# A new placement of the first two and a half batches of an attention and MLP kernel

## The chip, the cores and the metric

The kernel runs on one core of a Trainium2 chip. The metric is the time of one execution in microseconds (us) on the device. The engines of the core are named as the profile names them: PE (TensorE, matrix products; PEld is its weight load), DVE (VectorE), ACT (ScalarE), POOL (GpSimd) and SP (SyncE, which only issues transfers). Each engine takes its instructions in the order in which they were recorded, and waits at one whose input isn't there.

## The reference

For each of 8 batches and 8 heads, 576 positions are pooled into 32 memories, the queries attend to these, and the joined heads go through a two-layer MLP with a squared ReLU.

```python
a = phi - np.max(phi, axis=2, keepdims=True)     # phi: batch, head, 576, 32
a = np.exp(a)
a = a / (np.sum(a, axis=2, keepdims=True) + 1e-09)
k_m = np.einsum('bhsm,bhsd->bhmd', a, k)
v_m = np.einsum('bhsm,bhsd->bhmd', a, v)
scores = scale * np.matmul(q, k_m.transpose(0, 1, 3, 2))
scores = scores - np.max(scores, axis=-1, keepdims=True)
attn = np.exp(scores)
attn = attn / (np.sum(attn, axis=-1, keepdims=True) + 1e-09)
x = np.matmul(attn, v_m)                          # heads joined: 4608 x 512
h = np.maximum(x @ w_in, 0.0)                     # 512 -> 2048
out = h * h @ w_out                               # 2048 -> 512
```

## The kernel before

The MLP is the main loop. It has 256 steps: 8 batches, two halves of 288 positions (`t`), and 16 blocks of 128 hidden units (`f`). A step is `ffn1` (6 products into a PSUM tile `h`, line 566), ReLU and square on ACT (lines 568, 572, 577) and DVE (574), a subtraction on POOL (579) that gives the low part `g_lo`, and, two or three steps later, `ffn2` (line 595, 12 products into four PSUM tiles `acc`). In the first 16 steps the blocks f = 0 to 3 are not split, and `ffn2` is line 587. Values are split into a high and a low part of a faster format, which is why everything has a `_hi` and a `_lo`. The attention is folded into the MLP: `attend` makes the weights `a_hi`, `a_lo` of one half, and `make_u` multiplies `w_in` by the memories of the batch, so that `ffn1` is `u` times `a`.

What isn't the main loop is cut into generators, each with a list of places. The loop counts half steps, two in a step; at each of them the generators whose next place has come record their next piece. So the list `plan` sets, for the first two and a half batches, the order of the instructions on each engine; batches 3 to 7 follow a fixed list. The pieces are: `fetch_w_in`, `fetch_w_out` (a transfer of 512 KB of weights, which arrive as the bits of 8-byte numbers), `decode_in`, `decode_out` (two conversions on ACT, lines 479 and 482; three operations on DVE, 484, 486 and 489; one addition, line 496, on DVE or POOL as the plan says), `split_out`, `task_exp` (the softmax of phi), `task_mem` (the memories), `task_attend`, `task_u`, `task_stream` (transformed weights back from memory) and `task_spin` (a product that nobody reads).

`attend` has three passes over 128x576 numbers that may stand on DVE or POOL: subtracting the maximum (line 401), dividing by the sum (412), and the low part (419). The table `on_gpsimd` says which of the three are on POOL, by batch and half.

A single PSUM tile `ps_m` serves all the side work: each taker must find it released. `make_u` holds it from its products (line 372) through the copy `u_hi` on ACT (456) to the subtraction `u_lo` on DVE (458).

Before the loop, the string `order` gives the sequence of the pieces of batch 0 ("s" and `spin` being products without a reader), and `loads` the sequence of the first transfers. Almost all transfers are issued by SP, one after the other.

Of the kernel before, what the change touches and what calls it, by code (L numbers as in the profile page):

```python
# [24 lines left out]
def attn_moe_kernel(ctx: ExitStack, tc: tile.TileContext, qT, kv, phi, w_in, w_out, outT):  # L25
# [111 lines left out]
    def spin(n, x):  # L137

        h = ps_h.tile([P, 512], F32, name="h")
        for _ in range(n):  # L140
            nc.tensor.matmul(h, x, ident[:, None, :].broadcast_to([P, 4, P]), start=True, stop=True)

    def spin_r(*xs):

        h = ps_h.tile([P, 512], F32, name="h")
        for x in xs:
            for _ in range(4):
                nc.tensor.matmul(h[:, :T], turn[:, :P], x, start=True, stop=True)
# [578 lines left out]
    loads = [  # L727
        (first_phi,),
        (first_kv, 0),
        (first_kv, 1),  # L730
        (fetch_w_in, 0, 1),
        (fetch_w_in, 0, 0),
        (task_q, 0, 0),
        (task_q, 0, 1),
        (fetch_w_in, 1, 0),
        (fetch_w_in, 1, 1),
        (fetch_w_out, 0),
        (fetch_w_out, 1),
        (fetch_w_out, 4),
        (task_phi, 1),  # L740
        (next_kv,),
        (fetch_w_out, 2),
        (fetch_w_out, 5),
        (fetch_w_out, 6),
        (task_kv, 1, 0),
        (fetch_w_out, 3),
        (fetch_w_in, 3, 0),
        (fetch_w_in, 3, 1),
        (task_q, 1, 0),
        (fetch_w_in, 2, 1),  # L750
        (fetch_w_out, 7),
        (fetch_w_in, 2, 0),
    ]
    later = 10
# [35 lines left out]


    plan = [
        ((29, 29, 31), decode_in, 4, 0, nc.gpsimd),
        ((48, 53, 54), decode_in, 6, 0, nc.gpsimd),
        ((61,), task_kv, 2, 0),
        ((0, 1, 1), decode_out, 0, nc.gpsimd, True),
        ((6, 8, 10), decode_out, 3, nc.gpsimd, True),
        ((38, 43, 45), decode_in, 4, 1, nc.vector),
        ((110, 115), split_out, 0),
        ((5,), task_q, 1, 1),  # L800
        ((20,), fetch_w_in, 6, 1),
        ((90,), task_kv, 2, 1),
        ((0, 0, 2, 2, 3, 4), lambda: start["a1"]),
# [1 line left out]
        ((78, 81), split_out, 1),
        ((0, 1, 2), decode_out, 1, nc.gpsimd, True),
        ((47, 47, 49), decode_in, 6, 1, nc.vector),
        ((38,), fetch_w_out, 10),
        ((8,), fetch_w_in, 5, 0),
        ((62, 62, 64), decode_in, 7, 0, nc.vector),  # L810
        ((58, 59, 60), decode_in, 7, 1, nc.gpsimd),
        ((90,), task_stream, 2, 0),
        ((45, 46, 46, 48, 48), decode_out, 8, nc.vector),
        ((73, 73, 74), task_u, 0, 3),
        ((100, 101, 101, 102, 104, 107, 108), task_attend, 2, 0),
        ((52,), fetch_w_out, 13),
        ((0, 2, 2), task_u, 0, 0, HC, 2 * HC),
        ((92,), task_q, 2, 1),
        ((64, 66, 67, 68, 70), decode_out, 12, nc.vector),
        ((8, 9, 15), decode_in, 3, 0, nc.vector),  # L820
        ((16,), fetch_w_in, 4, 0),
        ((100,), task_stream, 2, 1),
# [1 line left out]
        ((35, 41, 41), decode_in, 5, 1, nc.vector),
        ((67,), fetch_w_out, 15),
        ((54, 56, 56, 58, 62), decode_out, 9, nc.vector),
        ((14, 14, 14, 17, 18, 18, 20), task_attend, 1, 1),
        ((73,), task_q, 2, 0),
        ((36,), fetch_w_out, 9),
        ((27,), fetch_w_out, 8),  # L830
        ((71,), fetch_w_out, 14),
        ((147,), task_stream, 2, 2),
        ((29, 29, 33, 35, 35), decode_out, 7, nc.gpsimd),
        ((49,), task_phi, 2),
        ((21, 22, 24, 27, 30), decode_out, 5, nc.gpsimd),
        ((68, 71, 71, 75, 77), decode_out, 13, nc.vector),
# [3 lines left out]
        ((3,), task_spin, 1),  # L840
        ((57,), fetch_w_out, 12),
        ((12,), fetch_w_in, 4, 1),
        ((9,), fetch_w_in, 7, 0),
        ((3,), task_spin, 1),
        ((105, 105, 105), task_u, 2, 0),
        ((109,), task_stream, 2, 3),
# [1 line left out]
        ((3, 8, 8), decode_out, 2, nc.gpsimd, True),
        ((92, 98), split_out, 2),
        ((110, 111, 113), task_u, 2, 1),  # L850
        ((11, 11, 14), task_u, 1, 0),
        ((7,), fetch_w_in, 5, 1),
        ((50, 51, 55), task_u, 0, 2),
# [2 lines left out]
        ((74, 75, 77, 79, 83), decode_out, 14, nc.gpsimd),
        ((14, 16, 19), decode_in, 2, 0, nc.gpsimd),
        ((14,), fetch_w_in, 6, 0),
        ((83, 84, 84, 86, 86), decode_out, 15, nc.gpsimd),
        ((118, 118, 120), task_u, 2, 2),  # L860
        ((100, 120), split_out, 3),
        ((10, 10, 10, 11, 11, 12, 12), task_attend, 1, 0),
        ((51, 55, 55, 58, 61), decode_out, 10, nc.vector),
        ((62, 62, 64), task_u, 1, 2),
        ((2, 4, 5, 6, 6, 6), task_exp, 1),
        ((28, 28, 28), task_u, 1, 1),
        ((38,), fetch_w_out, 11),
        ((76, 77, 77), task_u, 1, 3),
        ((32, 33, 33, 35, 37), decode_out, 6, nc.vector),
        ((62, 62, 64, 68, 70), decode_out, 11, nc.vector),  # L870
        ((20, 21, 23, 29, 29), decode_out, 4, nc.gpsimd),
        ((8, 8, 9, 9), task_mem, 1),
# [123 lines left out]
```

## Time and profile before

| | |
|---|---|
| time, median of 3 runs | 739.28 us (738.86 to 742.27) |
| time of the profiled execution | 739.42 us |
| its span, first to last instruction | 737.6 us |
| PE, PEld busy | 98%, 89% of the span |
| DVE, ACT, POOL busy | 51%, 48%, 36% |
| mean granted clock of TensorE | 0.995 of full speed |

The span and the time differ by 1.8 us, which lie around the instructions. A busy share is an average: the three side engines are nearly full in the first 150 us, when all weights are decoded, and far from it later.

### The profile page before, as it was taken

How to read it: one execution, taken by the hardware profiler on the slowest of the kernel's cores; microseconds unless marked ns; L12 is line 12 of the kernel's file. 1: busy time of each engine (PE TensorE's matmuls, PEld its weight loads, DVE VectorE, ACT ScalarE, POOL GpSimd, SP SyncE). 2: the span in 40 equal slices, each digit the busy share in tenths (PEclk: the TensorE clock that was granted, in tenths of full speed). 3: DMA queues.
4: the chain of work that ended last, by engine and by line, in shares of the span. 5: the costliest groups of instructions: out<-in, count | busy, mean ns of one | idle time of the engine just before them, and what ended most of it. 6: DMA issues, size and time to landing. Idle time of an engine off the chain costs nothing.

```text
span 737.6 us, 15709 instructions
## 1 busy us (share of the span) xinstructions
PE 721.2 (98%) x6170; PEld 655.1 (89%) x6170; DVE 379.6 (51%) x764; ACT 351.6 (48%) x750; POOL 263.8 (36%) x333
## 2 busy tenths in 40 slices
PE   8889999999999999999999999999999999999997
PEld 4467789889899898999899999899889999999997
DVE  4986779974565455254543556254542555321211
ACT  3546878874543344343544345433443435443332
POOL 1433334353443234332433324242333333333332
PEclk9999999999999999999999999999999999999999
DMA  9993228414429019131481216530391314100000
GB/s 306 354 363 117 105 67 265 147 30 125 140 76 313 25 56 298 44 122 34 143 222 44 80 33 244 122 121 2 87 281 31 122 34 147 58 33 1 33 2 32
DMA packets 64409, 89.61 MB, mean 121 GB/s; under 512 B 3984, under 2 KB 54928, under 8 KB 60752
## 3 DMA queue, kind: packets, MB, share of 16 engines
q1 hardware_dynamic: 63344, 87.34, 37.0%
q10 hardware_dynamic: 992, 1.28, 0.5%
q8 instruction: 48, 0.79, 0.4%
q14 instruction: 25, 0.20, 0.1%
HBM read 74.97 MB, written 13.63 MB: 120 GB/s over the span
## 4 chain that ended last, share of the span: by engine, by line
PE 83%; DVE 10%; ACT 4%; issue 1%; DMA 1%; POOL 1%; ACTq 0%; DVEq 0%; POOLq 0%
PE acc L595 49%; PE h L566 24%; PE ps_m L372 5%; PE ps_m L303 2%; DVE tmp L486 2%; DVE tmp L489 2%; PE acc L587 1%; DVE tmp L484 1%; DMA e_sb<-in_phi 1%; ACT low L482 1%; DVE u_lo L458 1%; ACT tmp L479 1%; DVE tmp L496 1%; ACT g L572 1%; ACT r L568 1%
## 5 line engine op out<-in xcount | busy, mean ns | idle before, releaser
L579 POOL TENSOR_TENSOR g_lo<-g,g_hi 128x288 fp32r<-128x288 f32 x240 | 202.4, 845 | 405.2 <-DVE g L574 313.3
L595 PE MATMUL acc<-g_hi,wo 128*128 128x288 f32 x1920 | 307.3, 298 | 0.4 <-DVE o L607 0.3
L595 PEld LDWEIGHTS acc<-g_hi,wo 128*128 128x128 f32 x1920 | 271.6, 188 | 25.3 <-ACT r L568 18.3
L574 DVE TENSOR_TENSOR g<-h,r 128x288 f32<-128x288 f32 x217 | 98.7, 456 | 307.3 <-ACT r L568 301.5
L568 ACT ACTIVATE r<-h 128x288 f32<-128x288 f32 x256 | 104.9, 410 | 295.0 <-PE h L566 286.4
L595 PE MATMUL acc<-g_lo,wo 128*128 128x288 f32 x960 | 176.5, 295 | 0.6 <-POOL g_lo L579 0.6
L595 PEld LDWEIGHTS acc<-g_lo,wo 128*128 128x128 f32 x960 | 144.2, 188 | 0.9 <-POOL g_lo L579 0.9
L577 ACT ACTIVATE g_hi<-r 128x288 fp32r<-128x288 f32 x240 | 106.5, 444 | 19.8 <-ACT r L568 0.8
L566 PE MATMUL h<-a_hi,u_hi 128*128 128x288 f32 x512 | 114.5, 305 | 0.7 <-ACT r L568 0.7
L566 PE MATMUL h<-a_hi,u_lo 128*128 128x288 f32 x512 | 109.8, 296 | 0.3 <-DVE u_lo L458 0.3
L566 PE MATMUL h<-a_lo,u_hi 128*128 128x288 f32 x512 | 109.6, 295 | 0.0
L566 PEld LDWEIGHTS h<-a_hi,u_hi 128*128 128x128 f32 x512 | 82.7, 188 | 10.5 <-issue 6.1
L566 PEld LDWEIGHTS h<-a_hi,u_lo 128*128 128x128 f32 x512 | 82.1, 188 | 0.5 <-DVE u_lo L458 0.5
L566 PEld LDWEIGHTS h<-a_lo,u_hi 128*128 128x128 f32 x512 | 82.2, 189 | 0.0
L458 DVE TENSOR_TENSOR u_lo<-ps_m,u_hi 128x1024 fp32r<-128x1024 f32 (+1 forms) x33 | 38.8, 1176 | 11.8 <-ACT u_hi L456 11.7
L372 PE MATMUL ps_m<-w_sb,mem 64*32 64x512 f32 (+1 forms) x528 | 37.1, 588 | 1.3 <-DVE w_sb L496 0.9
L587 PE MATMUL acc<-g_hi,wo 128*128 128x288 f32 x128 | 34.5, 414 | 1.7 <-POOL wo L496 1.7
L456 ACT CAST u_hi<-ps_m 128x1024 fp32r<-128x1024 f32 (+1 forms) x33 | 32.3, 980 | 5.0 <-PE ps_m L372 3.0
L587 PEld LDWEIGHTS acc<-g_hi,wo 128*128 128x128 f32 x128 | 23.6, 193 | 10.3 <-POOL wo L496 2.5
L482 ACT ACTIVATE low<-wo 128x512 int32<-128x512 uint32 x32 | 21.6, 674 | 8.6 <-DVE w_sb L496 4.4
L489 DVE SCALAR_TENSOR_TENSOR tmp<-wo,tmp 128x512 int32<-128x512 int32 x32 | 24.4, 761 | 1.1
L479 ACT ACTIVATE tmp<-wo 128x512 f32<-128x512 f32 x32 | 21.5, 672 | 4.4 <-DMA wo<-in_w_in 2.7
(136 smaller groups left out, 485.1 us busy)
## 6 DMA issues: line engine op xcount, KB each, us to landing
w_sb<-w_f SPq DMA_DIRECT2D x24, 1024.0 KB, 5.7
out_t<-o SPq DMA_DIRECT2D x62, 144.0 KB, 1.9
wo<-in_w_in SPq DMA_DIRECT2D x16, 512.0 KB, 8.3
wo<-in_w_out SPq DMA_DIRECT2D x16, 512.0 KB, 6.7
q_sb<-in_q SPq DMA_DIRECT2D x28, 288.0 KB, 3.4
kvb<-in_kv SPq DMA_DIRECT2D x28, 256.0 KB, 6.6
tmp<-in_kv SPq DMA_DIRECT2D x18, 256.0 KB, 6.0
w_f<-w_sb SPq DMA_DIRECT2D x4, 1024.0 KB, 7.6
```

The source lines that it names most:

```text
L372: nc.tensor.matmul(bank(out, half)[M * pr:M * (pr + 1), :y.shape[-1]], mem[hs, x, pr], y, start=True, stop=True)
L456: nc.scalar.copy(u_hi[:, :, n0:n1], ps[:, :, :n1 - n0])
L458: nc.vector.tensor_tensor(out=u_lo[:, :, n0:n1], in0=ps[:, :, :n1 - n0], in1=u_hi[:, :, n0:n1].bitcast(F32), op=ALU.subtract)
L482: nc.scalar.activation(r, word(0, U32), AF.Copy, scale=2.0 ** -29)
L489: nc.vector.scalar_tensor_tensor(out=c, in0=word(1, I32), scalar=-0x40000000, in1=c, op0=ALU.bitwise_and, op1=ALU.bitwise_or)
L566: nc.tensor.matmul(h[:, :T], u[:, qd, fs], x[:, qd], start=(i == 0), stop=(i == len(todo) - 1))
L568: nc.scalar.activation(r, h[:, :T], AF.Relu)
L574: nc.vector.tensor_tensor(out=g, in0=h[:, :T], in1=r, op=ALU.mult)
L577: nc.scalar.activation(g_hi, r, AF.Square)
L579: nc.gpsimd.tensor_tensor(out=g_lo, in0=g, in1=g_hi.bitcast(F32), op=ALU.subtract)
L587: nc.tensor.matmul(acc[e][:, :T], wo[f][:, e * P:(e + 1) * P], g_hi, start=first, stop=last)
L595: nc.tensor.matmul(acc[e][:, :T], wo[f][:, w, e * P:(e + 1) * P], x, start=first and x is g_hi and w == 0, stop=last and x is g_lo,)
```

## The change

Four things are changed. The transfers of `loads` stand in another order, 15 in place of 10 of them ahead of the loop's start. The places of nearly all pieces in `plan` are new, with some of the decoding additions changed between DVE and POOL (POOL has 18 of them, before 16). By the table `on_gpsimd`, ten passes of the six attentions of batches 0 to 2 stand on POOL, before fourteen. And the 28 products in float32r (`spin_r`) that nobody reads are gone, with the copy of 128x768 that fed them; five more `spin` stand in their place. Steps 35 to 38 square on DVE and no longer on ACT (`SQ_ACT`), and `ffn2` of step 9 comes ahead of `ffn1` of step 11.

```diff
-    def spin_r(*xs):
...
-            nc.scalar.copy(turn.rearrange("p (c x) -> p c x", c=3), e_sb[:, :3])
...
-    on_gpsimd = {(0, 0): (0, 1, 2), (0, 1): (0, 1, 2), (1, 0): (0, 1, 2), (1, 1): (0, 1), (2, 0): (1, 2), (2, 1): (0,)}
+    on_gpsimd = {(0, 0): (1, 2), (0, 1): (2,), (1, 0): (2,), (1, 1): (0, 1), (2, 0): (0, 2), (2, 1): (1, 2)}
...
-            spin_r(*(turn[:, i:i + T] for i in (0, 1, 2, 4)))
+            spin(2, ident)
             spin(2, mx[:, :1].broadcast_to([P, P]))
...
-            spin_r(turn[:, 8:8 + T], turn[:, :2 * T:2], turn[:, :1].broadcast_to([P, T]))
-            spin(1, sm[:, :1].broadcast_to([P, P]))
+            spin(2, sm[:, :1].broadcast_to([P, P]))
...
-    SQ_ACT = 39
+    SQ_ACT = 35
...
-        "e e e e e m m d0 m m d0 s d0 a0 a0 a1 d1 d1 a0 a0 d1 u0 d2 a0 d2 u0 a0 u0 d3 d3 d2 s d3 s d3 a0"
+        "e e e e e m m d0 m m s d0 a0 a0 d1 a0 a1 a0 d0 d1 d1 u0 d2 a0 s s d2 s a0 u0 d3 a0 d3 u0 d3 s d3 d2"
...
-        ((136, 142, 142), task_u, 2, 3),
+        ((128, 137, 137), task_u, 2, 3),
...
-        ((22, 23, 23), decode_in, 3, 1, nc.gpsimd),
+        ((22, 24, 25), decode_in, 3, 1, nc.gpsimd),
...
-        for _ in range({2: 1, 6: 1, 7: 1, 10: 1}.get(k, 0)):
+        for _ in range({2: 1, 6: 1, 7: 1, 10: 1, 11: 1}.get(k, 0)):
```

The new kernel is shorter, so its line numbers are smaller by 7 to 10: line 383 there is 391 of before, 393 is 401, 403 is 412.

The order on DVE is shown first where the attention of the second half of batch 0 follows on the decoding of the first blocks of w_out; `st`, `mx` and `sm` belong to the attention, `tmp` and `wo` to the decoding, and `at<-e_sb` begins the softmax of phi of batch 1. Before:

```order
L396 TENSOR_REDUCE mx<-st 128x18
L484 TENSOR_SCALAR tmp<-tmp 128x512
L486 TENSOR_SCALAR tmp<-tmp 128x512
L489 SCALAR_TENSOR_TENSOR tmp<-wo_133,tmp 128x512
L484 TENSOR_SCALAR tmp<-tmp 128x512
L486 TENSOR_SCALAR tmp<-tmp 128x512
L489 SCALAR_TENSOR_TENSOR tmp<-wo_391,tmp 128x512
L406 TENSOR_REDUCE sm<-st 128x18
L407 TENSOR_SCALAR sm<-sm 128x18
L408 RECIPROCAL sm<-sm 128x18
L458 TENSOR_TENSOR u_lo_333<-ps_m,u_hi_332 128x2x256
L173 TENSOR_TENSOR at<-e_sb 128x512
```

And with the change:

```order
L388 TENSOR_REDUCE mx<-st 128x18
L393 TENSOR_TENSOR st<-st,mx 128x576
L475 TENSOR_SCALAR tmp<-tmp 128x512
L477 TENSOR_SCALAR tmp<-tmp 128x512
L480 SCALAR_TENSOR_TENSOR tmp<-wo_135,tmp 128x512
L449 TENSOR_TENSOR u_lo_327<-ps_m,u_hi_326 128x2x256
L398 TENSOR_REDUCE sm<-st 128x18
L399 TENSOR_SCALAR sm<-sm 128x18
L400 RECIPROCAL sm<-sm 128x18
L403 TENSOR_TENSOR st<-st,sm 128x576
L166 TENSOR_TENSOR at<-e_sb 128x512
L167 TENSOR_TENSOR phi_mx<-at 128x256
```

The two passes `st<-st,mx` and `st<-st,sm` now stand on DVE, and one decoding instead of two lies between the maximum and the sum; the other one (of w_out block 1) comes after the maximum of phi.

On SP, the loads around phi of batch 1 (`e_sb`), its k and v (`u_hi`, `u_lo` for one half of the heads, `kvb` for the other) and the weights (`wo`). Before, from w_out block 1 on:

```order
L466 DMA wo_391<-in_w_out 128x512
L466 DMA wo_393<-in_w_out 128x512
L155 DMA e_sb<-in_phi 128x4x256
L159 DMA e_sb<-in_phi 64x256
L272 DMA u_hi_397<-in_kv 128x512 x2
L272 DMA u_lo_398<-in_kv 128x512 x2
L272 DMA u_hi_399<-in_kv 64x512
L466 DMA wo_406<-in_w_out 128x512
L466 DMA wo_408<-in_w_out 128x512
L466 DMA wo_410<-in_w_out 128x512
L272 DMA kvb_87<-in_kv 128x4x128
```

With the change, from w_out block 3 on:

```order
L457 DMA wo_143<-in_w_out 128x512
L457 DMA wo_377<-in_w_out 128x512
L264 DMA u_hi_379<-in_kv 128x512 x2
L264 DMA u_lo_380<-in_kv 128x512 x2
L264 DMA u_hi_381<-in_kv 64x512
L148 DMA e_sb<-in_phi 128x4x256
L152 DMA e_sb<-in_phi 64x256
L457 DMA wo_390<-in_w_out 128x512
L457 DMA wo_392<-in_w_out 128x512
L457 DMA wo_394<-in_w_in 128x512
L457 DMA wo_396<-in_w_in 128x512
L264 DMA kvb_87<-in_kv 128x4x128
```

Phi of batch 1 has moved behind five more blocks of weights (four of w_out, one of w_in) and one half of k and v, and w_out block 1 behind phi.

On DVE again, at the start of batch 3: `phi_mx`, `at`, `top` and `e_sb` are its softmax of phi, `u_lo` the last part of `u` of batch 2, `den` the end of the memories of batch 3, which take the same PSUM tile `ps_m`. Before:

```order
L237 TENSOR_TENSOR top<-top 32x8 x3
L239 COPY top<-top 32x8 x3
L574 TENSOR_TENSOR g<-h,r 128x288
L241 COPY at<-top 128x256
L242 STREAM_TRANSPOSE phi_mx<-at 128x256
L245 TENSOR_TENSOR e_sb<-e_sb,phi_mx 128x1024
L248 TENSOR_TENSOR e_sb<-e_sb,phi_mx 64x256
L574 TENSOR_TENSOR g<-h,r 128x288 x2
L458 TENSOR_TENSOR u_lo_3012<-ps_m,u_hi_3011 128x1024
L574 TENSOR_TENSOR g<-h,r 128x288
L312 TENSOR_SCALAR den<-ps_m 128x2
```

With the change:

```order
L226 TENSOR_REDUCE top<-at 128x8
L449 TENSOR_TENSOR u_lo_2861<-ps_m,u_hi_2860 128x1024
L229 TENSOR_TENSOR top<-top 32x8 x3
L231 COPY top<-top 32x8 x3
L565 TENSOR_TENSOR g<-h,r 128x288
L233 COPY at<-top 128x256
L234 STREAM_TRANSPOSE phi_mx<-at 128x256
L237 TENSOR_TENSOR e_sb<-e_sb,phi_mx 128x1024
L240 TENSOR_TENSOR e_sb<-e_sb,phi_mx 64x256
L565 TENSOR_TENSOR g<-h,r 128x288 x3
L304 TENSOR_SCALAR den<-ps_m 128x2
```

The subtraction `u_lo`, with which `ps_m` is released, stood after the softmax and stands now ahead of most of it.

## Rows read from the trace of the kernel before

**Rows 1.** The page: busy time by engine, and the chain that ended last.
```profile
PE 721.2 (98%) x6170; PEld 655.1 (89%) x6170; DVE 379.6 (51%) x764; ACT 351.6 (48%) x750; POOL 263.8 (36%) x333
...
PE 83%; DVE 10%; ACT 4%; issue 1%; DMA 1%; POOL 1%; ACTq 0%; DVEq 0%; POOLq 0%
```

**Rows 2.** Waits of TensorE, whole span: total us, times, longest us.
```profile
PE acc L587 <- POOL wo L496: 1.7, 1, 1.7
PE ps_m L303 <- DVE u_lo L458: 1.6, 1, 1.6
...
PE h L566 <- ACT r L568: 0.7, 1, 0.7
PE acc L595 <- POOL g_lo L579: 0.6, 1, 0.6
```

**Rows 3.** Timeline of DVE, 28 to 50: start us, us, instruction, [idle before].
```profile
30.76 0.84 DVE L391 STREAM_TRANSPOSE st<-acc 128x288 f32<-128x288 f32 x2
...
32.76 1.26 DVE L486 TENSOR_SCALAR tmp<-tmp 128x512 int32<-128x512 int32 x1
...
40.28 1.37 DVE L174 TENSOR_TENSOR phi_mx<-at 128x256 f32<-128x256 f32 x1
```

**Rows 4.** Timeline of POOL, the same stretch.
```profile
38.53 1.16 POOL L412 TENSOR_TENSOR st<-st,sm 128x576 f32<-128x576 f32 x1 [2.33 <-DVE sm L408]
39.65 1.71 POOL L496 TENSOR_TENSOR wo<-tmp,low 128x512 int32<-128x512 int32 x1
```

**Rows 5.** Line 401 by engine: duration ns min/median/max, first and last start us.
```profile
L401 DVE TENSOR_TENSOR st<-st,mx x11: 748/749/759, 187.2 to 623.5; 128x576 f32<-128x576 f32 x11
L401 POOL TENSOR_TENSOR st<-st,mx x5: 1159/1199/1471, 19.5 to 205.1; 128x576 f32<-128x576 f32 x5
```

**Rows 6.** Line 486 of DVE, 0 to 150; columns as in rows 5.
```profile
L486 DVE TENSOR_SCALAR tmp<-tmp x30: 426/427/1528, 16.4 to 145.7; 128x512 int32<-128x512 int32 x30
```

**Rows 7.** Line 173 of DVE, whole span; columns as in rows 5.
```profile
L173 DVE TENSOR_TENSOR at<-e_sb x7: 679/682/1390, 38.9 to 575.0; 128x512 f32<-128x512 f32 x7
```

**Rows 8.** Timeline of ACT, the same stretch.
```profile
33.77 0.68 ACT L403 ACTIVATE st<-st 128x576 f32<-128x576 f32 x1 [0.32 <-POOL st L401]
```

**Rows 9.** Timeline of PE, 20 to 55.
```profile
23.73 2.32 PE L148 MATMUL h<-wo 128*128 128x288 f32 x12
...
26.75 1.88 PE L141 MATMUL h<-ident 128*128 128x512 f32 x4
...
42.15 0.57 PE L187 MATMUL ps_m<-ident,phi_mx 128*128 128x128 f32 x2 [2.37 <-DVE phi_mx L176]
...
44.81 2.56 PE L587 MATMUL acc<-g_hi,wo 128*128 128x288 f32 x8
...
48.10 1.32 PE L303 MATMUL ps_m<-kvb,e_sb 128*32 128x130 f32 x40
...
50.80 2.21 PE L587 MATMUL acc<-g_hi,wo 128*128 128x288 f32 x8
```

**Rows 10.** Busy time by stretch: PE, PEld, DVE, ACT, POOL, PEclk, DMA share, GB/s.
```profile
0.00:30.00 30.00, 25.28 (x272) 14.35 (x272) 19.20 (x37) 11.56 (x22) 9.79 (x22) 0.94 0.97 329
30.00:40.00 10.00, 7.48 (x40) 4.08 (x40) 9.76 (x16) 6.01 (x12) 3.99 (x4) 1.00 1.07 318
40.00:50.00 10.00, 7.85 (x122) 7.10 (x126) 7.82 (x12) 5.85 (x12) 4.05 (x3) 0.83 1.04 400
```

**Rows 11.** Tile kvb, 25 to 50: its loads, and issue to landing.
```profile
L272 SPq DMA_DIRECT2D kvb<-in_kv x5: 540/601/2526, 28.9 to 33.2; - x5
...
DMA to landing us min/median/max: 7.4/7.9/8.5
```

**Rows 12.** Timeline of PE, 80 to 102: two runs of line 372.
```profile
81.82 1.93 PE L372 MATMUL ps_m<-w_sb,mem 64*32 64x512 f32 x16
...
100.54 1.09 PE L372 MATMUL ps_m<-w_sb,mem 64*32 64x512 f32 x16
```

**Rows 13.** Timeline of PE, 242 to 250.
```profile
244.72 1.32 PE L303 MATMUL ps_m<-kvb,e_sb 128*32 128x130 f32 x40 [1.60 <-DVE u_lo L458]
```

More of the change, by code (lines that the diff above doesn't have):

```diff
@@ L141, in spin @@
             nc.tensor.matmul(h, x, ident[:, None, :].broadcast_to([P, 4, P]), start=True, stop=True)
-    def spin_r(*xs):
[L145 to L148, printed above, removed]
     def load_phi(b, nc_q=nc.sync):
@@ L729, in attn_moe_kernel @@
         (first_kv, 0),
+        (task_q, 0, 0),
         (first_kv, 1),
+        (fetch_w_in, 0, 0),
         (fetch_w_in, 0, 1),
-        (fetch_w_in, 0, 0),
-        (task_q, 0, 0),
+        (fetch_w_in, 1, 0),
         (task_q, 0, 1),
-        (fetch_w_in, 1, 0),
+        (fetch_w_out, 2),
+        (fetch_w_out, 4),
+        (fetch_w_out, 0),
         (fetch_w_in, 1, 1),
-        (fetch_w_out, 0),
-        (fetch_w_out, 1),
[L739 to L743, printed above, removed]
+        (fetch_w_out, 5),
+        (fetch_w_in, 3, 0),
+        (fetch_w_out, 3),
+        (fetch_w_out, 7),
+        (next_kv,),
+        (task_phi, 1),
+        (fetch_w_out, 1),
         (fetch_w_out, 6),
+        (fetch_w_in, 2, 0),
+        (fetch_w_in, 3, 1),
         (task_kv, 1, 0),
-        (fetch_w_out, 3),
-        (fetch_w_in, 3, 0),
-        (fetch_w_in, 3, 1),
         (task_q, 1, 0),
         (fetch_w_in, 2, 1),
-        (fetch_w_out, 7),
-        (fetch_w_in, 2, 0),
     ]
-    later = 10
+    later = 15
     for fn, *args in loads[:later]:
@@ L760, in attn_moe_kernel @@
     spin(3, ident)
-    turn = const.tile([P, 3 * NQ * P], F32R, name=f"wo{NFT - 1}")
     start = {
@@ L792, in attn_moe_kernel @@
     plan = [
[L793 to L803, printed above, removed]
@@ L804, in attn_moe_kernel @@
-        ((50,), fetch_w_in, 7, 1),
[L805 to L822, printed above, removed]
-        ((40, 45, 46), task_u, 0, 1),
[L824 to L836, printed above, removed]
-        ((13, 17, 19), decode_in, 2, 1, nc.vector),
-        ((33, 35, 42), decode_in, 5, 0, nc.vector),
-        ((80, 83, 83, 84, 85, 87), task_exp, 2),
@@ L840, in attn_moe_kernel @@
[L840 to L846, printed above, removed]
-        ((136, 142, 142), task_u, 2, 3),
[L848 to L853, printed above, removed]
@@ L854, in attn_moe_kernel @@
-        ((92, 92, 93, 93), task_mem, 2),
-        ((108, 109, 112, 112, 114, 116, 118), task_attend, 2, 1),
[L856 to L872, printed above, removed]
-        ((22, 23, 23), decode_in, 3, 1, nc.gpsimd),
+        ((92, 99), split_out, 2),
@@ new lines, in attn_moe_kernel @@
+        ((15, 17, 19), decode_in, 2, 0, nc.vector),
+        ((76, 77, 78), task_u, 1, 3),
+        ((28, 29, 30), task_u, 1, 1),
+        ((3,), task_spin, 1),
+        ((53, 56, 56, 60, 61), decode_out, 9, nc.vector),
+        ((60,), fetch_w_out, 15),
+        ((0,), fetch_w_in, 4, 1),
+        ((107,), task_stream, 2, 3),
+        ((35, 41, 43), decode_in, 5, 1, nc.vector),
+        ((92, 92, 93, 93), task_mem, 2),
+        ((29, 30, 31), decode_in, 4, 0, nc.gpsimd),
+        ((54, 57, 59), decode_in, 6, 0, nc.gpsimd),
@@ new lines, in attn_moe_kernel @@
+        ((0,), fetch_w_in, 5, 0),
+        ((23, 24, 26, 31, 32), decode_out, 5, nc.gpsimd),
+        ((0, 2, 2), decode_out, 0, nc.gpsimd, True),
+        ((67,), fetch_w_out, 14),
+        ((11, 11, 14), task_u, 1, 0),
+        ((8, 8, 9, 9), task_mem, 1),
+        ((2,), fetch_w_in, 7, 0),
+        ((3, 3, 5), decode_out, 1, nc.gpsimd, True),
+        ((47, 47, 48), decode_in, 6, 1, nc.gpsimd),
+        ((50,), fetch_w_in, 7, 1),
+        ((62, 62, 62), decode_in, 7, 0, nc.vector),
+        ((49,), fetch_w_out, 10),
@@ new lines, in attn_moe_kernel @@
+        ((98,), task_stream, 2, 0),
+        ((71, 72, 74), task_u, 0, 3),
+        ((14, 14, 14, 16, 18, 19, 20), task_attend, 1, 1),
+        ((40, 45, 46), task_u, 0, 1),
+        ((61,), fetch_w_out, 13),
+        ((22, 24, 25), decode_in, 3, 1, nc.gpsimd),
+        ((103,), task_q, 2, 1),
+        ((67, 68, 69, 71, 75), decode_out, 12, nc.vector),
+        ((99,), task_stream, 2, 1),
+        ((25,), fetch_w_out, 8),
+        ((118,), task_stream, 2, 2),
+        ((28, 28, 31, 35, 35), decode_out, 7, nc.gpsimd),
@@ new lines, in attn_moe_kernel @@
+        ((3,), task_spin, 1),
+        ((76,), task_q, 2, 0),
+        ((40, 43, 43), decode_in, 4, 1, nc.vector),
+        ((32, 35, 39), decode_in, 5, 0, nc.gpsimd),
+        ((7, 7, 8), decode_out, 3, nc.gpsimd, True),
+        ((65,), task_phi, 2),
+        ((85,), task_kv, 2, 1),
+        ((95, 100, 100, 101, 103, 106, 109), task_attend, 2, 0),
+        ((0, 1, 2), task_u, 0, 0, HC, 2 * HC),
+        ((61, 61, 63), decode_in, 7, 1, nc.gpsimd),
+        ((10, 10, 10, 11, 11, 12, 12), task_attend, 1, 0),
@@ new lines, in attn_moe_kernel @@
+        ((61,), fetch_w_out, 12),
+        ((45, 46, 46, 48, 48), decode_out, 8, nc.gpsimd),
+        ((70, 71, 71, 78, 79), decode_out, 13, nc.gpsimd),
+        ((109, 109, 109), task_u, 2, 0),
+        ((74, 75, 77, 80, 83), decode_out, 14, nc.vector),
+        ((2,), fetch_w_in, 4, 0),
+        ((113, 113, 113), task_u, 2, 1),
+        ((59,), fetch_w_out, 11),
+        ((21,), fetch_w_in, 5, 1),
+        ((51, 56, 56, 58, 61), decode_out, 10, nc.vector),
+        ((97, 119), split_out, 3),
@@ new lines, in attn_moe_kernel @@
+        ((0, 7, 7), decode_out, 2, nc.vector, True),
+        ((81, 82, 82, 83, 83), decode_out, 15, nc.vector),
+        ((34,), fetch_w_out, 9),
+        ((76, 80), split_out, 1),
+        ((2,), fetch_w_in, 6, 0),
+        ((2, 4, 5, 6, 6, 6), task_exp, 1),
+        ((62, 63, 65), task_u, 1, 2),
+        ((62, 66, 66, 68, 70), decode_out, 11, nc.gpsimd),
+        ((32, 33, 33, 35, 37), decode_out, 6, nc.vector),
+        ((13, 17, 19), decode_in, 2, 1, nc.vector),
+        ((79, 82, 82, 84, 84, 87), task_exp, 2),
@@ L874, in attn_moe_kernel @@
+        ((8, 9, 17), decode_in, 3, 0, nc.vector),
+        ((77,), task_kv, 2, 0),
+        ((108, 109, 112, 112, 114, 116, 118), task_attend, 2, 1),
+        ((119, 122, 125), task_u, 2, 2),
+        ((36,), fetch_w_in, 6, 1),
+        ((104, 112), split_out, 0),
+        ((0,), task_q, 1, 1),
+        ((128, 137, 137), task_u, 2, 3),
+        ((0, 0, 2, 2, 6, 6), lambda: start["a1"]),
+        ((20, 21, 21, 29, 29), decode_out, 4, nc.gpsimd),
+        ((50, 50, 51), task_u, 0, 2),
     ]
```

## The prediction

> **What bounds the kernel now.** I read the page first. PE is busy for 98% of the span and makes up 83% of the chain that ended last; the rest of that chain is mostly DVE (10%) [rows 1]. So the time is PE's work plus what PE waits or runs slowly for. The change leaves the products of the main loop alone, so I looked for PE's losses and asked which of them the new placement reaches.
>
> The waits of PE [rows 2] are short, and of the long ones one stands early and one late: 1.7 us for the first decoded block of w_out, 2.37 us for the maximum of phi of batch 1 at 42.15 [rows 9], and 1.60 us at 244.72, where the memories of batch 3 want the PSUM tile that `u` of batch 2 still holds [rows 13]. The next ones are 0.7 and 0.6 us. One more is no wait in that view: the products of `u` that begin at 81.82 take 1.93 us, where the same ones take 1.09 us at 100.54 [rows 12]; the difference, 0.84 us, lies inside the group.
>
> The larger loss is the start. The stretch 30 to 40 has PE busy for 7.48 us, and 40 to 50 for 7.85 us at a mean granted clock of 0.83 [rows 10]. At the two levels of 1.2 and 2.4 GHz, 0.83 means about 3.4 of the 10 us at the lower one, which is 1.7 us of lost work; it stands behind the wait of 2.37 us. The engine that PE waits for there is DVE, busy for 9.76 of the 10 us from 30 to 40 [rows 10].
>
> Why is DVE so full? Its line 486 takes 0.43 us in the median and up to 1.53 [rows 6], line 173 takes 0.68 and once 1.39 [rows 7]. The long ones lie where POOL works: the maximum of phi, line 174, runs from 40.28 to 41.65 while POOL's addition runs from 39.65 to 41.36 [rows 3, 4]. At 32.76, line 486 takes 1.26 us [rows 3]. So a pass on POOL costs DVE up to 0.8 us while it runs, about as much as the 0.75 us for which DVE would do it itself, and on POOL it takes 1.20 us [rows 5].
>
> The Trainium skill says in "SBUF — State Buffer", section "Who interferes with whom", that the port pair is held for the whole instruction, and that whichever engine issues first blocks the other. This speaks against the change as well: a pass moved to DVE, with two inputs in SBUF, can hold up POOL's additions in turn. The trace agrees in one place, where POOL's addition takes 1.71 us [rows 4]. By that rule alone the four passes fewer on POOL would gain nothing at the start, and the sum below would lose its first term and come to 737.3.
>
> **The change part by part.** *Before 30.8 us: nothing.* The first half of batch 0 gets its subtraction on DVE, 0.75 us, in place of 1.20 on POOL and a hand-over; the exponential then starts when it did, since DVE does the same decoding meanwhile. The 12 products of `spin_r` that stood last took 2.32 us [rows 9]; in their place and in place of three spins behind them now stand six spins. Two take 1.88 us (four records, two to a product [rows 9]), so six take 5.6 us, against 2.3 + 2.8 before: `ffn1` of step 0 starts up to 1 us later. This is covered, because the next thing that PE needs is the decoded w_in from DVE, which comes at the same time: the transposition that follows it on DVE starts at 30.76 [rows 3], and I expect it there within 0.5 us. Without that cover it would cost the 1 us. The first half's low part may come 1 us later too, because its ACT copy stands behind a decoding whose weights now land later; it hides behind the same decoded w_in.
>
> *30.8 to 50.8: two limits.* First DVE. From 30.76 on it now does the transposition (0.84) and the maximum (0.75, as the pass has), the subtraction (0.75), one decoding (1.5, an estimate from three operations of which line 486 is one), then waits for the exponential. That was at 33.77 [rows 8]; two more activations stand ahead of it now, about 0.6 us each by the length of this one, so it ends near 35.6. The sum, reciprocal and second pass take 2 us: 37.6. DVE is then free for phi.
>
> Second, the transfers, which are saturated: 329, 318 and 400 GB/s in three stretches [rows 10]. Counted from `loads`, 12.32 MB stand in the queue up to the last part of `kvb` before, and 14.94 MB now. The last part was issued at 33.2 and took 7.4 us, so it landed at 40.6 [rows 11]; by the rates 13.3 MB had moved by then, 1.0 more than these. So now it lands when 15.9 MB have moved: 13.05 MB by 40, the rest at 400 GB/s, at 47.2. Phi of batch 1 (11.67 MB deep) lands in the same way near 38.7. Its maximum takes 0.68 us [rows 7] and two smaller operations of an estimated 0.4 without POOL beside it, so PE has it at 40.3 in place of 42.15: 1.9 us earlier. Then w_out block 1, which lands near 40.3, must be converted, decoded and added, 3.5 us, so `ffn2` of step 1 starts near 43.9 in place of 44.81 [rows 9], and the next `ffn1` is done about when the last `kvb` lands. The memories' products, which took from 48.10 to 50.80 [rows 9], end 1.4 us behind the last `kvb`: 48.6. That is 2.2 us earlier. If the transfers go on at 318 GB/s, `kvb` lands at 49.0 and 0.4 us are left; if the clock falls again, up to 1.7 us of work come on top, partly inside the wait for `kvb`. I take **2.0 us**, between 0 and 2.5; it is carried on, because the attention of batch 1 starts from these memories and its two moved passes are shorter.
>
> *50 to 240.* `u` of the second quarter waited 0.84 us for an addition of w_in. That addition is recorded two places later now (25 for 23), and the products at 28 as before, but POOL has two softmax passes fewer to do ahead of it. I take **0.4 us**, between 0 and 0.8. The two more additions on POOL, the four squares moved from ACT to DVE and all the new places can take away waits (0.7 + 0.6 us [rows 2] and smaller ones) or make new ones. No row shows them. Below stand the 1.3 us, above as much again and more; I take zero, since nearly every piece keeps its place within a few half steps.
>
> *244.* `u_lo` is recorded six half steps ahead of the memories of batch 3 in place of one (137 and 142, against 143). A copy and a subtraction don't reach over the three steps between, so the wait goes: **1.6 us**, or 0 if the transfer that feeds these products is late.
>
> *The rest* (batches 3 to 7) is the same list and costs the same.
>
> **Sum.** 739.42 - 2.0 - 0.4 - 1.6 = 735.4 in terms of the profiled execution, which lies 0.14 us above the median. Forecast: 735.3 us.
>
> **The rivals.** (a) *The forecast*, chance 0.45, with a range of its own of 733.5 to 736.8 (the first term from 1.0 to 2.5, the unknown waits 1 us either way).
> (b) *The load order eats the gain of the start.* Phi and w_out block 1 stand 3.3 MB and 4.9 MB deeper in the queue, and a rate of 318 GB/s, as from 30 to 40, is enough for it, or a clock that falls in the wait for `kvb`. Against it stands the 400 GB/s of the next stretch. Then 739.28 - 0.4 - 1.6 = 737.3; chance 0.2.
> (c) *The waits after 60 us go as well.* For it: they are short and each hangs on one placing. Then the 1.3 us and the other half of the 0.84 come off: 735.3 - 1.7 = 733.6, with a start that gains its full 2.5, 733.1; chance 0.2.
> (d) *The decoding becomes the bound, slower.* DVE already makes up a tenth of the chain that ended last and ACT 4% [rows 1], so where the chain lies on them, a longer one comes out of PE's time one for one. With 18 additions on POOL in place of 16, two more collisions of 0.8 us, and four more squares on DVE (an estimate of 0.4 each, half of a pass of [rows 5], which has twice the numbers): 3.2 us; if the chain doesn't start earlier either, 739.28 - 1.6 + 3.2 = 740.9. It is slower than before from a growth of 4 us over the forecast, and by over 0.5% from 7.8 us, which takes some five pieces late by one transfer. Chance 0.15, of which 0.09 beyond 0.5%.
> That the change doesn't do what it says is excluded: the rows of the order show the passes moved.
>
> **How the numbers follow.** Half a per cent, 3.7 us, is about what a measurement of this kernel can tell from no change: 735.6 and 743.0 are the limits. The forecast lies at the lower one; of its 0.45 I count 0.25 as faster and 0.2 as the same. With (c), faster is 0.45. The same: 0.2 + 0.2 from (b) + 0.06 from (d) = 0.46. Slower: 0.09. The range leaves out one in ten on each side: from 731.8, below (c) with some unknown waits gone, to 740.5, most of the way to (d).
>
> **What would show it.** Right: no wait of PE at 244; the maximum of phi reaching PE near 40.3; the products with `kvb` ending near 48.6, behind a wait for a transfer; line 486 at 0.43 us more often; the start of the first `ffn1` near 29. Wrong: a clock below 1.00 in more than one stretch after 20 us; waits of over 1 us of PE between 60 and 240, on ACT or POOL; `kvb` landing after 49.

## The result, and the profile after

The changed kernel takes 732.58 us in the median of 4 runs (732.32 to 733.08), the kernel before 739.15 beside it. The ratio is 0.990, interval 0.988 to 0.993: faster by 1.0%. The profiled execution took 732.32 us, 7.10 less than that of before. The gain is in three places, read from one event that both traces have, the ReLU of a step on ACT (line 568, after 559): at step 6 it starts 1.90 us earlier (59.22 for 61.12), at step 64 5.42 us earlier (218.17 for 223.59), and from step 72 to the end 7.10 us. So in this pair of profiles the start gave 1.9 us, the stretch from 60 to 224 us 3.5, and the beginning of batch 3 1.7.

The page of the changed kernel, parts 1 and 4, and its windows (PE, PEld, DVE, ACT, POOL busy, PEclk, DMA, GB/s); they answer to [rows 1, 10]:

```profile
PE 718.4 (98%) x6152; PEld 651.3 (89%) x6152; DVE 379.1 (52%) x771; ACT 350.0 (48%) x745; POOL 263.1 (36%) x330
...
PE 95%; DVE 2%; ACT 1%; DMA 1%; issue 0%; POOL 0%; ACTq 0%; DVEq 0%; POOLq 0%
```

```profile
30.00:40.00 10.00, 7.67 (x49) 4.94 (x50) 9.60 (x20) 6.75 (x14) 1.64 (x2) 1.00 1.06 355
40.00:50.00 10.00, 8.46 (x147) 6.47 (x146) 8.36 (x17) 6.22 (x12) 3.96 (x3) 1.00 1.07 324
```

Busy shares hardly move. What moves is the chain that ended last: PE from 83% to 95%, DVE from 10% to 2%. The timeline of PE after, for [rows 9, 12, 13]:

```profile
28.88 0.83 PE L557 MATMUL h<-a_hi,u_hi 128*128 128x288 f32 x2
...
39.19 0.38 PE L180 MATMUL ps_m<-ident,phi_mx 128*128 128x128 f32 x2
...
41.98 2.21 PE L578 MATMUL acc<-g_hi,wo 128*128 128x288 f32 x8 [0.36 <-POOL wo L487]
...
45.97 0.43 PE L295 MATMUL ps_m<-kvb,e_sb 128*32 128x130 f32 x8 [0.19 <-DMA kvb<-in_kv]
...
48.64 2.21 PE L578 MATMUL acc<-g_hi,wo 128*128 128x288 f32 x8
...
79.94 1.09 PE L364 MATMUL ps_m<-w_sb,mem 64*32 64x512 f32 x16
...
237.63 1.32 PE L295 MATMUL ps_m<-kvb,e_sb 128*32 128x130 f32 x40
```

The maximum of phi is there at 39.19 without a wait (before 2.37 us, at 42.15), the products with `kvb` end at 48.64, the products of `u` at 79.94 take 1.09 us in place of 1.93, and the memories of batch 3 wait for nothing. Waits of PE from 50 to 260, before and after (total us, times, longest):

```profile
PE ps_m L303 <- DVE u_lo L458: 1.6, 1, 1.6
PE h L566 <- ACT r L568: 0.7, 1, 0.7
PE acc L595 <- POOL g_lo L579: 0.6, 1, 0.6
PE acc L595 <- DVE o L607: 0.3, 1, 0.3
PE acc L595 <- ACT o L614: 0.2, 1, 0.2
```

```profile
PE acc L586 <- DVE o L598: 0.2, 1, 0.2
```

Without `u_lo`, which belongs to the beginning of batch 3, these rows name 1.6 of the 3.5 us in the middle (1.8 less the 0.2 that is left), and the products of `u` are 0.84. The other 1.1 us lie in no gap: from step 13 to step 64 PE stands idle for 1.75 us of 143.50 before and for 0.23 us of 139.90 after, so the rest of the difference is time in which the profile shows it busy, and which products take it was not located. The windows from 80 to 165, before and then after, show that the side engines do more in the same time, POOL most of all:

```profile
80.00:165.00 85.00, 83.25 (x621) 73.26 (x620) 69.52 (x108) 66.87 (x148) 35.58 (x35) 1.00 0.38 128
```

```profile
80.00:165.00 85.00, 84.77 (x652) 76.83 (x652) 72.51 (x113) 68.23 (x147) 43.57 (x45) 1.00 0.43 142
```

### The profile page after: what moved, and what is told of

Same layout as the page of the kernel before. It is cut to its first block, busy times and chain, and to the rows that moved or that the text cites. A ratio compares the mean times of both kernels' runs of the same rounds, so it can differ in the third digit from the quotient of the medians.

```text
span 730.5 us, 15675 instructions
## 1 busy us (share of the span) xinstructions
PE 718.4 (98%) x6152; PEld 651.3 (89%) x6152; DVE 379.1 (52%) x771; ACT 350.0 (48%) x745; POOL 263.1 (36%) x330
## 4 chain that ended last, share of the span: by engine, by line
PE 95%; DVE 2%; ACT 1%; DMA 1%; issue 0%; POOL 0%; ACTq 0%; DVEq 0%; POOLq 0%
PE acc L586 53%; PE h L557 28%; PE ps_m L364 6%; PE acc L578 4%; PE ps_m L295 2%; PE h L141 1%; DMA e_sb<-in_phi 1%; PE acc L295 0%; ACT tmp L470 0%; DVE tmp L480 0%; ACT low L473 0%; ACT r L559 0%; DVE tmp L477 0%; POOL w_sb L487 0%; DVE e_sb L202 0%
## 5 line engine op out<-in xcount | busy, mean ns | idle before, releaser
L570 POOL TENSOR_TENSOR g_lo<-g,g_hi 128x288 fp32r<-128x288 f32 x240 | 204.5, 854 | 393.5 <-DVE g L565 314.7
L565 DVE TENSOR_TENSOR g<-h,r 128x288 f32<-128x288 f32 x221 | 100.4, 456 | 303.5 <-ACT r L559 295.5
L578 PEld LDWEIGHTS acc<-g_hi,wo 128*128 128x128 f32 x128 | 23.2, 189 | 10.7 <-POOL wo L487 3.0
L410 POOL TENSOR_TENSOR a_lo<-at,a_hi 128x576 fp32r<-128x576 f32 x15 | 21.7, 1445 | 15.3 <-ACT a_hi L409 15.3
```

Of the source, the lines that this page charges most:

```text
L410: by(2).tensor_tensor(out=a_lo, in0=at, in1=a_hi.bitcast(F32), op=ALU.subtract)
L565: nc.vector.tensor_tensor(out=g, in0=h[:, :T], in1=r, op=ALU.mult)
L570: nc.gpsimd.tensor_tensor(out=g_lo, in0=g, in1=g_hi.bitcast(F32), op=ALU.subtract)
L578: nc.tensor.matmul(acc[e][:, :T], wo[f][:, e * P:(e + 1) * P], g_hi, start=first, stop=last)
```

## The experiments

Two theories for the start and the middle. The one of the prediction: fewer passes on POOL free DVE, and the phi transfer, early enough, does the rest. The rival: only the places in `plan` count, since they decide what stands ahead of what in each engine's queue.

### The passes alone, and the new plan alone

The kernel before with one line of the change:

```diff
-    on_gpsimd = {(0, 0): (0, 1, 2), (0, 1): (0, 1, 2), (1, 0): (0, 1, 2), (1, 1): (0, 1), (2, 0): (1, 2), (2, 1): (0,)}
+    on_gpsimd = {(0, 0): (1, 2), (0, 1): (2,), (1, 0): (2,), (1, 1): (0, 1), (2, 0): (0, 2), (2, 1): (1, 2)}
```

> The kernel before with only the new table of passes on POOL. Theory P (the passes freed DVE and with it the whole decoding, so they made the gain between 50 and 160 us): start 1.0 us earlier, middle 2.5 us shorter, about 735.5 us. Theory L (the new places in the list made that gain): the start gains at most 1.0 us, the middle nothing, 738.2 to 739.

Measured: 740.45 us, ratio 1.0007 (0.9995 to 1.0019). The passes alone give nothing that can be measured, and the trace suggests why. DVE's line 486, 0 to 60, grouped (instructions | busy us, mean ns | idle us before), and the window 0 to 60 (columns as above), of the kernel before and then, in the same two views, with the passes moved:

```profile
L486 DVE TENSOR_SCALAR tmp<-tmp 128x512 int32<-128x512 int32 x9 | 8.4, 934 | 0.3
```

```profile
0.00:60.00 60.00, 50.58 (x525) 32.22 (x525) 43.16 (x76) 28.97 (x55) 20.26 (x30) 0.94 0.97 331
```

```profile
L486 DVE TENSOR_SCALAR tmp<-tmp 128x512 int32<-128x512 int32 x9 | 6.8, 757 | 0.3
```

```profile
0.00:60.00 60.00, 51.34 (x524) 31.52 (x525) 43.17 (x81) 28.81 (x55) 15.44 (x26) 0.97 0.96 331
```

The collisions become fewer (934 to 757 ns in the mean), but DVE is busy for 43.17 us in place of 43.16: it does itself what it lost to them. The prediction took from the section of the Trainium skill that it names ("SBUF — State Buffer", "Who interferes with whom") that the passes would gain nothing. This run agrees in the result. It doesn't show the way that the prediction gave for it, that DVE holds up POOL's additions in turn: of the six additions up to 60 us one is long in either trace, 1.71 us before and 1.66 with the passes moved.

What decides when phi's maximum comes is the stretch on DVE that ends with it, from the transposition of the second half of batch 0 on. Its two ends before, with the passes moved, and in the changed kernel:

```profile
30.76 0.84 DVE L391 STREAM_TRANSPOSE st<-acc 128x288 f32<-128x288 f32 x2
...
41.68 0.42 DVE L176 TENSOR_TENSOR phi_mx<-phi_mx,e_sb 64x256 f32<-64x256 f32 x1
```

```profile
32.24 0.84 DVE L391 STREAM_TRANSPOSE st<-acc 128x288 f32<-128x288 f32 x2
...
42.91 0.42 DVE L176 TENSOR_TENSOR phi_mx<-phi_mx,e_sb 64x256 f32<-64x256 f32 x1
```

```profile
30.87 0.83 DVE L383 STREAM_TRANSPOSE st<-acc 128x288 f32<-128x288 f32 x2
...
38.58 0.42 DVE L169 TENSOR_TENSOR phi_mx<-phi_mx,e_sb 64x256 f32<-64x256 f32 x1
```

From the start of the one to the start of the other these are 10.9, 10.7 and 7.7 us. In the six traces of this document with two decodings in the stretch it is 10.7 to 10.9 us, in the eight with one 7.6 to 8.7, wherever the passes stand.

And the kernel before with the list `plan`, `SQ_ACT` and the place of one `ffn2`:

```diff
-        ((22, 23, 23), decode_in, 3, 1, nc.gpsimd),
+        ((22, 24, 25), decode_in, 3, 1, nc.gpsimd),
...
-    SQ_ACT = 39
+    SQ_ACT = 35
...
-        for _ in range({2: 1, 6: 1, 7: 1, 10: 1}.get(k, 0)):
+        for _ in range({2: 1, 6: 1, 7: 1, 10: 1, 11: 1}.get(k, 0)):
```

> The kernel before with only the new list of places (with steps 35 to 38 squared on DVE and ffn2 of step 9 ahead of ffn1 of step 11). Theory L: 3.5 us in the middle and 1.6 us at the start of batch 3 come off, about 734.2 us. Theory P: only the 1.6 us, about 737.5 us.

Measured: 732.55 us, ratio 0.989 (0.987 to 0.991). The list, with the two small edits, carries the whole gain, 1.7 us more than theory L, which gave it nothing at the start.

### The change with the old passes, and with the old load order

```diff
-    later = 15
+    later = 10
```

with `loads` in its old order in the second; in the first `on_gpsimd` of before.

> The changed kernel with the old table of passes. Theory P: 1 us lost at the start and 2.5 us in the middle, about 736 us. Theory L: up to 1 us at the start, partly behind the wait for the last kvb, nothing later, 732.6 to 733.6 us.

> The changed kernel with the old order of loads: phi, w_out block 1 and kvb of batch 1 land 9, 14 and 6 us earlier, so PE has no wait for kvb near 46. If the new order of loads is what limits its start: 0.7 to 1.2 us faster than the changed kernel, about 731.6 us. If the new order is needed by the new places (a decoding that waits for its weights): slower than the changed kernel, 734 us or more. If neither: 732.6 us.

Measured: 732.89 us, 0.989 (0.988 to 0.991), and 732.40 us, 0.989 (0.987 to 0.990). Neither part is needed. With the old load order the last `kvb` lands at 40.1 us and PE doesn't wait for it (with the new one at 46.7): step 6 lies 2.37 us ahead of before, with the new one 1.90.

### Half of the list

The new places of decoding and transfers alone (with their adder engines and the sequence of the new list), with the old ones of the computing pieces (`u`, `attend`, the softmax of phi, the splits); and the other way round. From the two lists:

```diff
-        ((62, 62, 64, 68, 70), decode_out, 11, nc.vector),
+        ((62, 66, 66, 68, 70), decode_out, 11, nc.gpsimd),
...
-        ((28, 28, 28), task_u, 1, 1),
+        ((28, 29, 30), task_u, 1, 1),
```

> The kernel before with the changed kernel's sequence of the list plan and its places and adder engines for the decoding and for all transfers, but its own old places for u, attend, the softmax of phi, the memories and the splits, so the wait at 244 us stays. Theory D (the middle 3.5 to 4 us come from where the decoding and its transfers stand): 3.5 to 4 us under the kernel before, ratio 0.995, half step lag -3.5 to -4 from 165 us on and no more at 244. Rival C (they come from the places of the compute pieces): no change, ratio 1.000, lag under 1 us. Both fall if it is a matter of the two together: then slower than before.

> The kernel before with the changed kernel's places of u, attend, the softmax of phi, the memories and the splits alone; decoding and transfers where they stood. All expect 1.6 us from u_lo ahead of the memories of batch 3, with the wait of PE at 244 gone. Theory D: nothing else, ratio 0.9978, and a lag of 0 up to 240 us. Rival C: 3.5 us more, ratio 0.993.

Measured: 743.9 us, ratio 1.0045 (1.003 to 1.006), and 748.6 us, 1.011 (1.008 to 1.013). Both theories of these runs fall: each half makes the kernel slower. The decoding half does bring a gain in the middle, 2.35 us between step 13 and step 40, but its profile begins the middle 2.55 us late (PE waits for w_out block 1 for 1.44 us at 44.62, and from 40 to 50 the granted clock is 0.69), and the first of the waits below takes another 2.7. Waits of PE from 50 to 260, the two longest of each; first the decoding half, then the computing half:

```profile
PE ps_m L195 <- DVE nmx L190: 2.8, 1, 2.8
PE ps_m L303 <- DVE u_lo L458: 1.6, 1, 1.6
```

```profile
PE h L566 <- DVE u_lo L458: 4.4, 1, 4.4
PE ps_m L372 <- DMA w_sb<-w_f: 2.2, 1, 2.2
```

Each wait of these is one piece that stands behind another: with the decoding moved, `nmx` of batch 2 stands behind a whole decoding; with `u` moved, `u_lo` at 93.68 stands behind two decodings and a split, and the transformed weights, read back at their old place, come 2.2 us late. PE's products behind the wait of 4.4 us then ran at the lower of the clock's levels, as the timeline and the window 95 to 100 show (granted clock 0.50, that is 1.2 of 2.4 GHz):

```profile
94.95 0.85 PE L566 MATMUL h<-a_hi,u_lo 128*128 128x288 f32 x2 [4.41 <-DVE u_lo L458]
...
96.08 4.04 PE L587 MATMUL acc<-g_hi,wo 128*128 128x288 f32 x8
```

```profile
95.00:100.00 5.00, 5.00 (x13) 3.86 (x14) 1.84 (x2) 3.01 (x7) 2.22 (x2) 0.50 0.01 2
```

These eight products take 2.10 us at 88.18 in the same trace. The wait at 244 us is gone in the computing half: there its steps come 1.67 us closer to those of before, all that was expected of `u_lo`.

### Only the adder engines, and the second conversion later

Nine additions (the expectation says eleven) change their engine, no place moves; and the conversion into `low` recorded one place later:

```diff
-        ((62, 62, 64, 68, 70), decode_out, 11, nc.vector),
+        ((62, 62, 64, 68, 70), decode_out, 11, nc.gpsimd),
```

> The kernel before with only the adder engines of the changed kernel: eleven decoding additions change between DVE and POOL, no place moves. Theory E (the middle gain is which engine adds): 2 to 4 us faster, ratio 0.995 to 0.997. Rival (it is the places): within 0.7 us, ratio 0.999 to 1.001, and the waits of ACT for the buffer low stay at 7 us or more between 62 and 160.

Measured: 739.04 us, ratio 0.999 (0.998 to 1.000). The rival holds: the wait for `g_lo` at 148 us (0.63 us) is gone, the one for `o` grew from 0.3 to 0.6, and what is left can't be told from no change.

```diff
+        yield
         r = work.tile([P, n], I32, name="low", bufs=2)
         nc.scalar.activation(r, word(0, U32), AF.Copy, scale=2.0 ** -29)
-        yield
```

> The kernel before with the second conversion of every decoding (the one into the buffer low) recorded one place later, next to the DVE operations, so that ACT asks for the two low buffers later and stands less often in its queue waiting for an addition. Theory Q (ACT waiting in its queue for low, with the ReLU of the next step behind it, is what PE lost in the middle): waits of ACT at low between 62 and 160 fall from 7 us to under 3, and 2 to 4 us are gained, ratio 0.995 to 0.997. Rival (it is not that buffer): the waits fall and the time stays, ratio 0.999 to 1.001. Slower, if the later conversion makes the additions late.

Measured: 739.84 us, ratio 1.0003 (0.999 to 1.002). Waits of ACT from 62 to 160, before and then with the conversion later:

```profile
ACT low L482 <- DVE w_sb L496: 4.4, 3, 1.6
ACT r L568 <- PE h L566: 4.1, 3, 2.2
ACT low L482 <- DVE tmp L496: 2.7, 1, 2.7
```

```profile
ACT r L568 <- PE h L566: 7.3, 9, 2.3
ACT wo L553 <- DVE tmp L496: 4.6, 3, 1.8
ACT wo L553 <- POOL tmp L496: 1.8, 1, 1.8
...
ACT low L483 <- DVE tmp L496: 0.8, 1, 0.8
```

The waits at `low` fall from 7.9 us to 1.1. ACT waits for the same additions at its next instruction that needs them, the split (line 553; 6.4 us in place of 3.3), and then longer for PE's products (7.3 us in place of 4.1). The buffer was no cause; theory Q falls.

### Four entries

Which pieces stand badly is seen at 81.8 us in the kernel before [rows 12]. Its timelines of DVE and of POOL there:

```profile
80.53 0.69 DVE L489 SCALAR_TENSOR_TENSOR tmp<-wo,tmp 128x512 int32<-128x512 int32 x1
```

```profile
81.37 1.27 POOL L496 TENSOR_TENSOR w_sb<-tmp,low 128x512 int32<-128x512 int32 x1 [2.69 <-ACT o L614]
```

and POOL in the changed kernel:

```profile
78.49 1.33 POOL L487 TENSOR_TENSOR w_sb<-tmp,low 128x512 int32<-128x512 int32 x1 [1.62 <-ACT g_hi L563]
...
80.97 1.29 POOL L487 TENSOR_TENSOR tmp<-tmp,low 128x512 int32<-128x512 int32 x1 [1.15 <-DVE tmp L480]
```

`w_sb` is the last part of w_in that `u` needs. Before, it is decoded third, behind w_out blocks 4 and 5, and added from 81.37, while `u` already begins at 81.82. After, it is second and done at 79.82, ahead of the products at 79.94. So the kernel before with these entries alone:

```diff
-        ((21, 22, 24, 27, 30), decode_out, 5, nc.gpsimd),
+        ((23, 24, 26, 31, 32), decode_out, 5, nc.gpsimd),
...
-        ((136, 142, 142), task_u, 2, 3),
+        ((128, 137, 137), task_u, 2, 3),
...
-        ((20, 21, 23, 29, 29), decode_out, 4, nc.gpsimd),
+        ((20, 21, 21, 29, 29), decode_out, 4, nc.gpsimd),
...
-        ((22, 23, 23), decode_in, 3, 1, nc.gpsimd),
+        ((22, 24, 25), decode_in, 3, 1, nc.gpsimd),
```

> The kernel before with four entries of plan changed and nothing else: decode_in 3,1 and decode_out 4 and 5 take the places of the changed kernel, so that the last part of w_in of the second quarter is decoded ahead of w_out block 5 and not behind it, and u(2,3) takes (128,137,137). Theory (each wait is one piece standing behind another in a queue, and can be taken away alone): the products at 81.8 us fall from 1.93 to 1.09 us, the wait at 244 goes, 0.84 + 1.6 = 2.4 us, ratio 0.9967. Rival (the pieces of plan hang together, as the two halves of the list did, so the piece that is moved back makes a wait of its own): the products at 81.8 take 1.09 us, but a new wait of 0.8 us or more stands between 85 and 110, ratio 0.998 to 1.001.

Measured: 736.82 us, ratio 0.996 (0.994 to 0.998), 3.0 us; the 2.4 that were expected lie inside the interval. Its timelines of PE and of POOL there:

```profile
81.62 1.09 PE L372 MATMUL ps_m<-w_sb,mem 64*32 64x512 f32 x16
```

```profile
79.91 1.33 POOL L496 TENSOR_TENSOR w_sb<-tmp,low 128x512 int32<-128x512 int32 x1 [1.16 <-ACT r L568]
```

The addition is done before `u` starts. Against the kernel before, step 13 lies 0.06 us later, step 64 2.15 us earlier, and what follows the memories of batch 3 3.84 us earlier: 2.2 us of the middle's 3.5 and all of the 1.7. The wait for `r` at 99 us went as well; by which of the entries was not taken apart. Here a piece could be moved alone; the rival falls for these four.

### The list without the small edits, the old start, and one more version

```diff
-    SQ_ACT = 35
+    SQ_ACT = 39
...
-        for _ in range({2: 1, 6: 1, 7: 1, 10: 1, 11: 1}.get(k, 0)):
+        for _ in range({2: 1, 6: 1, 7: 1, 10: 1}.get(k, 0)):
```

> The kernel before with the whole list plan of the changed kernel, but squares on ACT up to step 38 as before and ffn2 of step 9 behind ffn1 of step 11 as before. If these two small edits carry nothing: 732.6, ratio 0.989 as with them. If the squares matter, since ACT is the fullest side engine from 140 to 156 us, where they stand: a wait of PE of about 0.8 us near 145, on g_lo or r, as before; ratio 0.990 to 0.991.

Measured: 732.15 us, ratio 0.990 (0.989 to 0.992): the list carries it without them. The next has `order` of before (its line is in the diff of the change), the last

```diff
-        "d2": lambda: decode_in(1, 0, nc.vector),
+        "d2": lambda: decode_in(1, 0),
```

on top of the old load order.

> The changed kernel with the old string order ahead of the loop; new load order, passes, plan and spins stay. If the gain of the start (1.9 us at step 6) is the sequence of the pieces on DVE and ACT there: 1.9 us slower than the changed kernel, 734.5, ratio 0.9928. If it is the spins, which no longer use the float32r copy, or the phi transfer: 732.6, ratio 0.990, lag at step 6 to 13 still -1.9.

Measured: 731.91 us, ratio 0.989 (0.988 to 0.991); step 6 lies 2.03 us ahead of before, as with the new `order`. So of the two theories the first, 734.5, falls: the gain of the start isn't in that string.

> The changed kernel with the old load order, 10 of the loads ahead of the loop, and the addition of one part of w_in (the first half of the second block) on POOL in place of DVE, where DVE has no pause from 26 to 46 us and POOL is idle from 29 to 35. The load order alone gave 732.4. If DVE's work bounds the start: 0.3 to 0.6 us less, 731.9, ratio 0.988, the transposition at 30.8 half a us earlier. If POOL's addition holds DVE up by as much as it takes over: the same 732.4, ratio 0.9886.

Measured: 732.20 us, ratio 0.990 (0.989 to 0.991). No gain over the load order alone. The six versions that contain the new list lie between 731.9 and 732.9; none can be told from the changed kernel.

## Why the prediction was right in sign and too small

Forecast 735.3, measured 732.58: inside the whole range (731.8 to 740.5), beyond the forecast's own (733.5 to 736.8). The terms:

- *Before 30.8 us, nothing.* Right: the first `ffn1` came at 28.88, 0.8 us later, and was covered.
- *30.8 to 50.8: 2.0 us.* Right in size: 1.9 here, and 1.7 in the mean of the seven traces with the new list (0.35 to 2.44). The sum for DVE was right: free for phi at 37.6, measured 37.41. The sum for the transfers came out too late. It put phi at 38.7 and the last `kvb` at 47.2, by the rates of the kernel before; they landed at 37.0 and 46.7, since 345 GB/s moved up to 30 us and 355 from 30 to 40 (329 and 318 before). So the maximum reached PE at 39.19 for 40.3, limited by DVE and not by the transfer. That the products with `kvb` still ended at 48.64 for 48.6 was luck: they took 2.0 us behind the last landing in place of 1.4.

  Its origin was half wrong too. I put the relief on the passes as much as on the decoding. With the passes alone step 6 came 0.1 us later than before, and `loads` and `order` were not needed. What stays is the list: `decode_out` of w_out block 1 stands behind the maximum of phi, so that one decoding less lies ahead of it. No run moves this piece alone, but the stretch on DVE above follows the number of decodings in every trace. It isn't the whole of the start: in the decoding half of the list it is 7.9 us, and PE is late there all the same.
- *50 to 240: 0.4 us.* **This step failed.** It measured 3.5. The term had two parts. For `u` of the second quarter I looked at the place of the addition (25 for 23, so later) and at POOL. What counts is what stands ahead of the piece in DVE's queue: w_out block 5 moved from 21 to 23 and fell behind it. With the four entries 2.2 us went; the 0.84 and the wait for `r` at 99 us (0.65) are 1.5 of them. For the rest I took zero because "nearly every piece keeps its place within a few half steps". A shift of two half steps is enough to let a decoding overtake another, as the two halves of the list show from the other side (waits of 2.8 and 4.4 us). The remaining 1.3 us are left to the other entries; the adder engines explain the wait at 148 us, and the rest was not taken apart, so its cause stays open.
- *244: 1.6 us.* Right: 1.68, and `u_lo` alone does it.

So rival (c), waits after 60 us that go as well, is what happened in kind, with the first term at 2.0; but it had 1.7 us more for the middle than the forecast, and 3.1 came. Of rival (b) little is seen: the products with `kvb` waited for 0.2 and 0.4 us. Rival (d) had no part: the chain on DVE shrank from 10% to 2%. It counted two more additions on POOL, as the text on the change does; the list and the trace have one more, 17 for 16.

Two readings of the rows were loose. "The next ones are 0.7 and 0.6 us" passes over three waits of 1.5, 1.4 and 0.9 us in the first 31 us, which the change was not meant to reach and mostly left (1.4, 1.4 and 0.6). And a pass on POOL costs DVE not "up to 0.8 us" but 1.1, by the longest row of line 486 (1.53 for 0.43).

## What to carry to other kernels

With in-order queues, read a change of places as an order: for each wait of the bound engine list the pieces ahead of the late one on its producer's queue, before and after, and price the ones that overtake. A place that is later can be earlier in the queue. Work moved off an engine to end collisions bought nothing here, where the engine that took it was the full one; look at the busy time of that engine, not at the durations that recover.
